# Keeping part of the input in SBUF between two passes, with the rest streamed through small slots

## The chip, the cores and the metric

One core of a Trainium2 chip. The metric is the device time of one execution in microseconds.

## The reference

```python
# x: (1, 384, 384, 384) bf16, channels last; w1d: (1,) bf16
g = jnp.einsum("bhwc->bc", x) / (H * W)     # mean of each channel
s = sigmoid(g * w1d[0])                     # k = 1: one weight for all channels
return x * s[:, None, None, :]
```

Every output needs a sum over the whole of x, so x (113 MB) has to pass through the core before the first output can be made. The four buffers that the kernel has in SBUF hold 25.2 MB of it.

## The kernel before

The 147,456 rows of 384 channels are cut in 18 tiles of 128 partitions x 64 rows, 6.29 MB each (48 KiB per partition). Four buffers hold one tile each. In the first pass TensorE sums each tile into PSUM by 64 matmuls with a matrix of ones. In the second all 18 tiles are loaded again, multiplied in place on VectorE and stored. Cuts are marked `# ...`.

```python
T = 18; n = 64; nbufs = 4; NL = 2 * T
# SyncE: all loads of both passes, in one loop
for i in range(NL):
    t = i % T; b = i % nbufs; k = i // nbufs
    if k >= 1:
        # wait until PE (first pass) or the store (second pass) has freed bufs[b]
        # ...
    sp.dma_start(bufs[b][:, :], xt[t]).then_inc(sem_ld[b], 16)

# TensorE: for each tile, once loaded
for r in range(n):
    ins = pe.matmul(psum_sums, ones_mat, bufs[b][:, r*C:(r+1)*C], start=..., stop=...)
ins.then_inc(sem_pe, 1)

# ScalarE: after the last tile
act.activation(s_b, psum_sums, Sigmoid, scale=wb_sb).then_inc(sem_sb, 1)
for t in range(T):
    act.wait_ge(sem_mul, t + 1)
    act.dma_start(ot[t], bufs[b][:, :]).then_inc(sem_st[b], 16)

# VectorE
for t in range(T):
    dve.wait_ge(sem_ld[b], 16 * (k + 1))      # t == 0 also waits for sem_sb
    dve.tensor_tensor(buf3, buf3, s_bc, mult).then_inc(sem_mul, 1)   # 128 x 24576
```

## Time and profile before

| | before |
|---|---|
| time | 798.71 us, median of 4 runs (798.19 to 798.87) |
| span of the profiled run | 796.1 us |
| HBM read, written | 226.5 MB, 113.2 MB |
| DMA share in both passes | 1.00, at 431 GB/s |
| VectorE busy | 233.4 us (29%) |

The span is the time from the first to the last instruction in the profile; the measured time of that same run was 797.84, 1.7 us more. The DMA share is the mean busy share of the core's 16 DMA engines. The prediction below shows the lines themselves.

### The profile page before, as it was taken

The page shows a single profiled execution, that of the slowest core. Times are in us where ns is not written, and L with a number is a line of the kernel's source. Part 1 is how long each engine was busy: PE and PEld are TensorE (multiplying, and loading weights), DVE is VectorE, ACT ScalarE, POOL GpSimd, SP SyncE. Part 2 cuts the span into 40 slices and gives each one's busy share as a digit, 9 for nine tenths or more (in the row PEclk, how much of TensorE's full clock was granted, in tenths as well). Part 3 has the DMA queues.
Part 4 walks back from the last instruction along what each step waited for, and adds up shares of the span by engine and source line. Part 5 has one row for each costly group of instructions (what it writes and reads, how often), then busy time and mean ns, then how long its engine had stood idle before and what let it go on. Part 6 is the DMA issues. An engine that isn't in the chain of part 4 may idle for free.

```text
span 796.1 us, 2417 instructions
## 1 busy us (share of the span) xinstructions
PE 209.6 (26%) x1153; PEld 117.8 (15%) x1153; DVE 233.4 (29%) x19; ACT 2.1 (0%) x3; POOL 0.5 (0%) x6
## 2 busy tenths in 40 slices
PE   0977887877878800000000000000000000000000
PEld 0534544544534400000000000000000000000000
DVE  0000000000000066624624623633632641651560
ACT  0000000000000000000000000000000000000000
POOL 0000000000000000000000000000000000000000
PEclk9989989989989965555555555555555555555555
DMA  9999999999999999999999999999999999999997
GB/s 385 436 435 431 433 435 428 428 432 433 428 430 433 428 432 435 435 435 435 427 425 435 430 435 432 427 435 427 435 425 430 427 435 435 435 432 435 432 395 326
DMA packets 7787, 339.89 MB, mean 427 GB/s; under 512 B 866, under 2 KB 866, under 8 KB 866
## 3 DMA queue, kind: packets, MB, share of 16 engines
q1 hardware_dynamic: 5186, 226.49, 66.3%
q10 hardware_dynamic: 2592, 113.25, 32.9%
q8 instruction: 9, 0.15, 0.1%
HBM read 226.49 MB, written 113.25 MB: 427 GB/s over the span
## 4 chain that ended last, share of the span: by engine, by line
another core or an unknown queue 33%; DMA 30%; DVE 28%; PE 7%; SPq 0%; issue 0%
DMA buf<-in_x_dram 30%; DVE buf L129 28%; PE psum_sums L101 7%; SPq L82 0%; SPq L70 0%
## 5 line engine op out<-in xcount | busy, mean ns | idle before, releaser
L129 DVE TENSOR_TENSOR buf<-buf,s_b 128x24576 bf16<-128x24576 bf16 x18 | 233.2, 12958 | 540.9 <-DMA buf<-in_x_dram 540.9
L101 PE MATMUL psum_sums<-buf,ones_mat 128*128 128x384 bf16 x1152 | 209.4, 347 | 66.5 <-DMA buf<-in_x_dram 66.5
L101 PEld LDWEIGHTS psum_sums<-buf,ones_mat 128*128 128x128 bf16 x1152 | 117.7, 103 | 157.9 <-DMA buf<-in_x_dram 73.1
L142 ACT ACTIVATE s_b<-psum_sums,wb_sb 128x384 bf16<-128x384 f32 x1 | 0.6, 580 | 275.5 <-PE psum_sums L101 275.5
L136 ACT ACT_TABLE_LOAD x1 | 1.3, 1283 | 0.7 <-PEq L169 0.7
L113 DVE TENSOR_SCALAR wb_sb<-psum_w 128x1 f32<-128x1 f32 x1 | 0.2, 159 | 2.2 <-PE psum_w L88 2.2
L88 PE MATMUL psum_w<-w_sb,ones_row 1*128 1x1 bf16 x1 | 0.2, 182 | 2.0 <-DMA w_sb<-in_w1d_dram 2.0
L88 PEld LDWEIGHTS psum_w<-w_sb,ones_row 1*128 1x128 bf16 x1 | 0.1, 100 | 2.0 <-DMA w_sb<-in_w1d_dram 2.0
L65 POOL MEMSET ones_mat<- 128x128 bf16 x1 | 0.2, 204 | 0.3 <-POOLq L169 0.3
L136 ACT ACTIVATE junk<-wb_sb 1x1 f32<-1x1 f32 x1 | 0.2, 202 | 0.4 <-DVE wb_sb L113 0.4
L66 POOL MEMSET ones_row<- 1x128 bf16 x1 | 0.2, 194 | 0.0
L169 POOL MEMSET const-bfloat16-1.0<- 128x1 bf16 x1 | 0.1, 106 | 0.0
L169 POOL MEMSET const-float32-0.0<- 128x1 f32 x1 | 0.1, 103 | 0.2 <-issue 0.2
L169 POOL MEMSET const-float32-1.0<- 128x1 f32 x1 | 0.1, 103 | 0.0
L169 POOL MEMSET const-uint8-127<- 128x1 uint8 x1 | 0.1, 103 | 0.0
## 6 DMA issues: line engine op xcount, KB each, us to landing
buf<-in_x_dram SPq DMA_DIRECT2D x36, 6144.0 KB, 49.0
out_dram<-buf ACTq DMA_DIRECT2D x18, 6144.0 KB, 50.6
w_sb<-in_w1d_dram SPq DMA_DIRECT2D x1, 0.0 KB
```

Source lines behind the costliest of these rows:

```text
L65: pool.memset(ones_mat[:, :], 1.0)
L66: pool.memset(ones_row[:, :], 1.0).then_inc(sem_ones, 1)
L88: pe.matmul(psum_w[:, 0:1], ones_row[0:1, :], w_sb[0:1, 0:1], start=True, stop=True,).then_inc(sem_wmm, 1)
L101: ins = pe.matmul(psum_sums[:, :], ones_mat[:, :], bufs[b][:, r * C:(r + 1) * C], start=(t == 0 and r == 0), stop=(t == T - 1 and r == n - 1),
L113: dve.tensor_scalar(wb_sb[:, 0:1], psum_w[:, 0:1], 1.0 / float(HW), None, mybir.AluOpType.mult,).then_inc(sem_wb, 1)
L129: dve.tensor_tensor(buf3, buf3, s_bc, mybir.AluOpType.mult).then_inc(sem_mul, 1)
L136: act.activation(junk[0:1, 0:1], wb_sb[0:1, 0:1], mybir.ActivationFunctionType.Sigmoid,)
L142: act.activation(s_b[:, :], psum_sums[:, :], mybir.ActivationFunctionType.Sigmoid, scale=wb_sb[:, 0:1],).then_inc(sem_sb, 1)
L169: nc = _bacc.Bacc("TRN2", target_bir_lowering=False, num_devices=1)
```

## The change

The first pass ends with tiles 14 to 17 in the four buffers. The change keeps them there instead of reading them again. The remainder of x must still be streamed through something, so an extra buffer of 16 rows and the first 48 rows of tile 14's buffer become four slots of 16 rows. All second-pass work is done in pieces of 16 rows (1.57 MB): first 13 resident pieces, which are only multiplied and stored, then 59 streamed ones. The last tile of the first pass is loaded in four quarters, so that TensorE need not wait for the whole of it. The diff, cut to its core:

```diff
-_NBUFS = 4
+_H = 16
+_N_STREAM = 4
+extra = es.enter_context(nc.sbuf_tensor("extra", [P, piece * C], bf16))
+slots = [extra[:, i * h * C:(i + 1) * h * C] for i in range(piece // h)]
+while len(slots) < _N_STREAM:
+    slots.append(pbuf[:, cut * C:(cut + h) * C]); cut += h
 # SyncE
-for i in range(NL): ...                       # 36 loads of a tile
+for t in range(T):                            # 18 tiles, the last in quarters
+    if t >= nb: sp.wait_ge(sem_pe, t - nb + 1)
+    # ...
+for u, (src, _d) in enumerate(stream):        # 59 pieces
+    s = u % ns
+    if u == n_extra: sp.wait_ge(sem_pe, part + 1)   # tile 14 has been summed
+    if u >= ns: sp.wait_ge(sem_st[s], 16 * (u // ns))
+    sp.dma_start(slots[s], src).then_inc(sem_sl[s], 16)
 # TensorE
+if t == T - 1 and r % piece == 0:
+    pe.wait_ge(sem_last[r // piece], 16)
 # VectorE: 13 resident pieces, then 59 streamed ones, 128 x 6144 each
-dve.tensor_tensor(buf3, buf3, s_bc, mult)
+for buf, r, k, _d in res:            dve.tensor_tensor(v, v, sbc(k), mult)
+for u in range(len(stream)): # ...   dve.tensor_tensor(v, v, sbc(h), mult)
 # ScalarE: stores of the same pieces in the same order
```

More of the change, by code (lines that the diff above doesn't have):

```diff
@@ L20, in bass_standalone__channel_attn_eca__vision_kernel @@
     n = _N_ROWS
-    nbufs = _NBUFS
+    h = _H
+    piece = 16
+    nb = 4
     assert S % (P * n) == 0
@@ L24, in bass_standalone__channel_attn_eca__vision_kernel @@
     HW = H * W
-    xt = x.rearrange("b h w c -> (b h w) c").rearrange(
-        "(t p k) c -> t p (k c)", p=P, k=n
-    )
-    ot = out.rearrange("b h w c -> (b h w) c").rearrange(
-        "(t p k) c -> t p (k c)", p=P, k=n
-    )
+    xr = x.rearrange("b h w c -> (b h w) c")
+    orr = out.rearrange("b h w c -> (b h w) c")
+    xt = xr.rearrange("(t p k) c -> t p (k c)", p=P, k=n)
+    ot = orr.rearrange("(t p k) c -> t p (k c)", p=P, k=n)
+    xs = xr.rearrange("(t p k) c -> t p (k c)", p=P, k=h)
+    os_ = orr.rearrange("(t p k) c -> t p (k c)", p=P, k=h)
     w2 = w1d.rearrange("(a b) -> a b", a=1)
-    NL = 2 * T
     with ExitStack() as es:
@@ L44, in bass_standalone__channel_attn_eca__vision_kernel @@
         psum_w = es.enter_context(nc.psum_tensor("psum_w", [P, 1], mybir.dt.float32))
-        sem_ld = [es.enter_context(nc.semaphore(f"sem_ld{i}")) for i in range(nbufs)]
-        sem_st = [es.enter_context(nc.semaphore(f"sem_st{i}")) for i in range(nbufs)]
+        bufs = [
+            es.enter_context(nc.sbuf_tensor(f"buf{i}", [P, n * C], mybir.dt.bfloat16))
+            for i in range(nb)
+        ]
+        extra = es.enter_context(nc.sbuf_tensor("extra", [P, piece * C], mybir.dt.bfloat16))
+        part = T - nb
+        pbuf = bufs[part % nb]
+        slots = [extra[:, i * h * C:(i + 1) * h * C] for i in range(piece // h)]
+        cut = 0
+        while len(slots) < _N_STREAM:
+            slots.append(pbuf[:, cut * C:(cut + h) * C])
+            cut += h
+        ns = len(slots)
+        n_extra = piece // h
+        stream = [(xs[u], os_[u]) for u in range(part * n // h)]
+        for r in range(0, cut, h):
+            stream.append((xt[part][:, r * C:(r + h) * C], ot[part][:, r * C:(r + h) * C]))
+        res = []
+        for t in range(part, T):
+            r = cut if t == part else 0
+            while r < n:
+                k = min(piece, n - r)
+                res.append((bufs[t % nb], r, k, ot[t][:, r * C:(r + k) * C]))
+                r += k
+        sem_ld = [es.enter_context(nc.semaphore(f"sem_ld{i}")) for i in range(nb)]
+        n_last = n // piece
+        sem_last = [es.enter_context(nc.semaphore(f"sem_la{i}")) for i in range(n_last)]
+        sem_sl = [es.enter_context(nc.semaphore(f"sem_sl{i}")) for i in range(ns)]
+        sem_st = [es.enter_context(nc.semaphore(f"sem_st{i}")) for i in range(ns)]
+        sem_rst = es.enter_context(nc.semaphore("sem_rst"))
         sem_wdma = es.enter_context(nc.semaphore("sem_wdma"))
@@ L53, in bass_standalone__channel_attn_eca__vision_kernel, with sbc @@
         sem_mul = es.enter_context(nc.semaphore("sem_mul"))
-        bufs = [
-            es.enter_context(nc.sbuf_tensor(f"buf{ib}", [P, n * C], mybir.dt.bfloat16))
-            for ib in range(nbufs)
-        ]
-        n_st_slot = [sum(1 for i in range(T, NL) if i % nbufs == b) for b in range(nbufs)]
+        def sbc(k):
+            return s_b[:, None, :].broadcast_to([P, k, C])
         with nc.Block() as block:
@@ L70, in _ @@
                 sp.dma_start(w_sb[:, :], w2[0:1, 0:1]).then_inc(sem_wdma, 16)
-                for i in range(NL):
-                    t = i % T
-                    b = i % nbufs
-                    k = i // nbufs
-                    if k >= 1:
-                        prev = i - nbufs
-                        if prev < T:
-                            sp.wait_ge(sem_pe, prev + 1)
-                        else:
-                            j = sum(1 for ii in range(T, prev + 1) if ii % nbufs == b)
-                            sp.wait_ge(sem_st[b], 16 * j)
-                    sp.dma_start(bufs[b][:, :], xt[t]).then_inc(sem_ld[b], 16)
+                for t in range(T):
+                    b = t % nb
+                    if t >= nb:
+                        sp.wait_ge(sem_pe, t - nb + 1)
+                    if t < T - 1:
+                        sp.dma_start(bufs[b][:, :], xt[t]).then_inc(sem_ld[b], 16)
+                    else:
+                        for q in range(n_last):
+                            lo, hi = q * piece * C, (q + 1) * piece * C
+                            sp.dma_start(
+                                bufs[b][:, lo:hi], xt[t][:, lo:hi]
+                            ).then_inc(sem_last[q], 16)
+                for u, (src, _d) in enumerate(stream):
+                    s = u % ns
+                    if u == n_extra:
+                        sp.wait_ge(sem_pe, part + 1)
+                    if u >= ns:
+                        sp.wait_ge(sem_st[s], 16 * (u // ns))
+                    sp.dma_start(slots[s], src).then_inc(sem_sl[s], 16)
             @block.tensor
@@ L95, in _ @@
                 for t in range(T):
-                    b = t % nbufs
-                    k = t // nbufs
-                    pe.wait_ge(sem_ld[b], 16 * (k + 1))
+                    b = t % nb
+                    if t < T - 1:
+                        pe.wait_ge(sem_ld[b], 16 * (t // nb + 1))
                     ins = None
                     for r in range(n):
+                        if t == T - 1 and r % piece == 0:
+                            pe.wait_ge(sem_last[r // piece], 16)
                         ins = pe.matmul(
@@ L119, in _ @@
                 ).then_inc(sem_wb, 1)
-                s_bc = s_b[:, None, :].broadcast_to([P, n, C])
-                for t in range(T):
-                    i = T + t
-                    b = i % nbufs
-                    k = i // nbufs
-                    dve.wait_ge(sem_ld[b], 16 * (k + 1))
-                    if t == 0:
-                        dve.wait_ge(sem_sb, 1)
-                    buf3 = bufs[b][:, :].rearrange("p (k c) -> p k c", k=n)
-                    dve.tensor_tensor(
-                        buf3, buf3, s_bc, mybir.AluOpType.mult
+                dve.wait_ge(sem_sb, 1)
+                for t in range(part, T - 1):
+                    dve.wait_ge(sem_ld[t % nb], 16 * (t // nb + 1))
+                for q in range(n_last):
+                    dve.wait_ge(sem_last[q], 16)
+                for buf, r, k, _d in res:
+                    v = buf[:, r * C:(r + k) * C].rearrange("p (k c) -> p k c", k=k)
+                    dve.tensor_tensor(
+                        v, v, sbc(k), mybir.AluOpType.mult
+                    ).then_inc(sem_mul, 1)
+                for u in range(len(stream)):
+                    s = u % ns
+                    dve.wait_ge(sem_sl[s], 16 * (u // ns + 1))
+                    v = slots[s].rearrange("p (k c) -> p k c", k=h)
+                    dve.tensor_tensor(
+                        v, v, sbc(h), mybir.AluOpType.mult
                     ).then_inc(sem_mul, 1)
@@ L147, in _ @@
                 ).then_inc(sem_sb, 1)
-                for t in range(T):
-                    i = T + t
-                    b = i % nbufs
-                    act.wait_ge(sem_mul, t + 1)
-                    act.dma_start(ot[t], bufs[b][:, :]).then_inc(sem_st[b], 16)
-                for b in range(nbufs):
-                    if n_st_slot[b] > 0:
-                        act.wait_ge(sem_st[b], 16 * n_st_slot[b])
+                j = 0
+                for buf, r, k, dst in res:
+                    j += 1
+                    act.wait_ge(sem_mul, j)
+                    act.dma_start(dst, buf[:, r * C:(r + k) * C]).then_inc(sem_rst, 16)
+                for u, (_s, dst) in enumerate(stream):
+                    s = u % ns
+                    j += 1
+                    act.wait_ge(sem_mul, j)
+                    act.dma_start(dst, slots[s]).then_inc(sem_st[s], 16)
+                act.wait_ge(sem_rst, 16 * len(res))
+                for s in range(ns):
+                    act.wait_ge(sem_st[s], 16 * len(range(s, len(stream), ns)))
 _INS = ['x', 'w1d']
```

## The prediction

> **What bounds the kernel now.** I began with the page's slices and its DMA lines, since a kernel that reads x twice and writes it once has only a multiplication per element to do.
>
> ```profile
> PE 209.6 (26%) x1153; PEld 117.8 (15%) x1153; DVE 233.4 (29%) x19; ACT 2.1 (0%) x3; POOL 0.5 (0%) x6
> ...
> DMA  9999999999999999999999999999999999999997
> GB/s 385 436 435 431 433 435 428 428 432 433 428 430 433 428 432 435 435 435 435 427 425 435 430 435 432 427 435 427 435 425 430 427 435 435 435 432 435 432 395 326
> DMA packets 7787, 339.89 MB, mean 427 GB/s; under 512 B 866, under 2 KB 866, under 8 KB 866
> ...
> HBM read 226.49 MB, written 113.25 MB: 427 GB/s over the span
> ```
>
> No engine is busy for a third of the span, while the DMA row is full from the first slice to the last but one, at the same rate in both passes. 427 GB/s over 796.1 us is all 339.9 MB: x read twice (2 x 113.25), the result written once. Next I read the chain in order of time, to get the period of the second pass:
>
> ```profile
> 705.49 0.02 issue
> 705.51 12.96 DVE buf L129
> 718.47 16.01 another core or an unknown queue
> 734.48 0.02 issue
> 734.50 12.96 DVE buf L129
> 747.46 16.02 another core or an unknown queue
> 763.48 0.02 issue
> 763.50 12.96 DVE buf L129
> ```
>
> A multiplication starts every 29.0 us and takes 12.96, so VectorE rests 16 us of each period. One period loads 6.29 MB and stores 6.29 MB: 12.58 MB / 29.0 us = 434 GB/s. The chain gives VectorE 28% of the span, but only because its line stands between one transfer and the next; with both queues kept full, a faster VectorE would gain nothing. Last, the windows over the first pass, the second, and the two parts of the end (columns: the window, its length, busy us of PE, PEld, DVE, ACT, POOL, clock, DMA share, GB/s):
>
> ```profile
> 2.00:264.00 262.00, 197.98 (x1084) 111.15 (x1085) 0.16 (x1) 0.22 (x2) 0.00 (x0) 0.92 1.00 431
> 310.00:764.00 454.00, 0.00 (x0) 0.00 (x0) 195.81 (x17) 0.00 (x0) 0.00 (x0) 0.50 1.00 431
> 764.00:777.00 13.00, 0.00 (x0) 0.00 (x0) 12.46 (x1) 0.00 (x0) 0.00 (x0) 0.50 0.80 348
> 777.00:797.00 20.00, 0.00 (x0) 0.00 (x0) 0.00 (x0) 0.00 (x0) 0.00 (x0) 0.50 0.75 324
> ```
>
> DMA share is 1.00 in both passes. Only at the end, from the last load's landing at 763.5, are the engines partly idle: 0.20 x 13 + 0.25 x 20 = 7.6 us. So the time is bytes over about 434 GB/s, plus a small head and tail.
>
> [...] The new pieces are 1.57 MB[...]. The trace has no transfer of that size, but it shows that a completion costs nothing while others are queued: 6.29 MB transfers end every 14.5 us in the first pass, with no idle share between. [...] the change needs 4 x 48 + 12 = 204 KiB plus about 1.5 for the small tensors[...].
>
> **The change part by part.** Call 16 rows per partition a piece: 128 x 12288 B = 1.573 MB, a quarter of a tile. x has 18 x 4 = 72 pieces.
>
> Removed: the last four tiles stay in their buffers after the first pass, except the first 48 rows of tile 14, whose place serves with the extra buffer as four streaming slots. Resident are 16 - 3 = 13 pieces; 14 x 4 + 3 = 59 are read again. Saved: 13 x 1.573 = 20.4 MB of 339.7, or 6.0%. At 434 GB/s that is 47.1 us of DMA time, all of it on the bounding resource.
>
> Added: smaller packets. The packet records of the trace have one packet per partition: 49152 B in 1815 ns (median), and the 4-byte semaphore write at the end of each transfer in 9 ns. Eight packets per DMA engine and one semaphore write make 8 x 1815 + 9 = 14.53 us per tile, which is the 14.5 us at which tiles land. My estimate for a 12288 B packet takes 9 ns as fixed and the rest as bytes: 1806/4 + 9 = 460 ns; a piece takes 8 x 460 + 9 = 3.69 us, against 3.63 for a quarter tile: 1.7% more.
>
> The sum of DMA time: 17 whole tiles x 14.53 = 247.0 us. Pieces: 4 (the last tile comes in four) + 59 loads + 72 stores = 135 x 3.69 = 498.2. Together 745.2; with 2.0 us before the first data, 747.2. The same sum for the kernel before is 54 x 14.53 + 2.0 = 786.6 against a span of 796.1, so 9.5 us lie beside it: 7.6 in the tail and some 2 in slow packets.
>
> Moved: the seam between the passes. The last load lands near 265 us, PE then needs one piece (16 matmuls at 10.57/64 = 0.165 us = 2.6 us) and not a whole tile, the sigmoid 0.6, [...] the issue about 1: the first store begins some 8 us after the last load. Meanwhile the four streaming loads stand in the queue (the extra buffer is free from the start, the three others once PE has done tile 14), 4 x 3.69 = 14.8 us of work. No bubble. Then 13 resident pieces: VectorE makes one per 3.36 + 0.05, DMA stores one per 3.69, so the store queue never empties, though by only 8%.
>
> Streaming: a slot's round is load 3.69, [...] multiplication 3.36, issue about 1, store 3.69, [...]: some 16 us unloaded [...]. DMA needs 2 x 3.69 = 7.4 us per piece, four slots 29.5. 29.5 against 16: almost twice what it takes to keep DMA busy. About three transfers should stand in the queues at any time.
>
> The tail: after the last load one multiplication of 3.4 us instead of 13, with earlier stores still running beside it, so the 2.6 us of idle DMA there shrink to 1 or less; the last transfer's stragglers and receipt remain, 3 us. Slow packets: 2 us before, [...] I take 4 in all. Span: 747.2 + 4 + 4 = 755. The measured time is 798.71 - 796.1 = 2.6 above the span: 758.
>
> **The rivals.** (1) Turnover of slots becomes the bound[...] I give it 4% in full and expect at most a trace of it. (2) Engines drift apart. In the landing records of the second pass, the 16 engines' parts of one load come up to 10 us apart, which buffers of 6.29 MB absorb; four slots hold about 11 us of work per engine, so a straggler may hold up a slot and leave others dry. A loss of 3% in the 400 us of streaming would be 12 us: 770. (3) VectorE bounds the resident stretch: if a piece took 4 us instead of 3.4, 13 x 0.3 = 4 us more: 762. The trace's fixed durations (all 18 at 12.96) speak against it. (4) Smaller packets cost nothing: 135 x 0.06 = 9 us less: 749. (5) The saved reads were hidden anyway: then 797; a DMA share of 1.00 in the very stretch where they fell excludes it.
>
> **Range and chances.** Rivals 2 and 3 push up, 4 down; so 748 to 774 about 758. Within 2% of 798.7 (above 783) it comes only if streaming loses over 25 us, rival 2 doubled or rival 1 in part: 6%. Slower by 2% needs rival 1 in full: 2%.
>
> **What would show it.** HBM read should be 206.1 MB, written 113.25. The DMA row should be full from end to end, the rate 425 to 430 in the second pass; 12288 B packets near 460 ns. VectorE: 72 multiplications of 3.36 us. The first resident store soon after 275 us, streaming loads landed near 281, resident stores done near 326, then 7.4 us per piece. I am wrong if the DMA row shows 7s and 8s in the streaming stretch with VectorE and both queues waiting by turns (rival 1 or 2), or if the rate falls at a full share (a packet cost mis-sized).

The trace of the kernel before has no multiplication of 16 rows and does not show a slot's round of 16 us. r_after has 3358 ns for the first (59 streamed pieces, mean), the 3.36 of the text. The 16 was the author's estimate; the steps that the text names with their times add up to 11.7 us. In the kernel before, the last load lands at 763.48, 0.06 us after its last packet, and the multiplication starts at 763.50; the last store lands 0.33 us after its last packet. Below, e3 gives the steps of a whole round.

## The result, and the profile after

Ratios are the mean time of one kernel's fast runs over that of the other's of the same rounds, so not quite the ratio of the medians that are quoted.

| | before | changed |
|---|---|---|
| median | 798.42 us (15 runs) | 751.59 us (10 runs, 8 fast) |
| fast runs | 796.09 to 800.29 | 750.15 to 754.56 |
| ratio of fast runs | 1 | 0.9413, 95% interval 0.9401 to 0.9426 |

The change is 5.9% faster, within the range. Executions over 1.5% slower than the fastest of the same kernel are left out of the means. Two of the ten runs were slow: 778.1 us at a mean granted clock of 0.571, which is the run that was profiled, and one of 1204.0 us at a clock of 1.0. The second was not profiled and never came again; nothing here explains it. So the same kernel was profiled again (the run r_after), and that profile is read here.

Its page, in the rows that answer to those shown for before:

```profile
PE 209.7 (28%) x1153; PEld 118.0 (16%) x1153; DVE 240.5 (32%) x73; ACT 2.1 (0%) x3; POOL 0.5 (0%) x6
...
DMA  9999999999999999999999999999999999999998
GB/s 377 435 438 423 440 433 423 440 438 420 435 438 423 413 404 426 423 428 400 429 430 430 430 430 430 431 430 430 431 430 430 430 430 430 431 430 430 429 430 373
DMA packets 21902, 319.47 MB, mean 426 GB/s; under 512 B 2434, under 2 KB 2434, under 8 KB 2434
...
HBM read 206.05 MB, written 113.25 MB: 425 GB/s over the span
```

The DMA row is as full as before, the mean rate is the same (426 against 427 GB/s), and 20.4 MB less were read. 20.4 of 339.9 MB is 6.0%; the span went from 796.1 to 750.5, 5.7%. The change left the kernel's bound where it was and gave it less to do.

The streaming stretch, from the timeline (start, length, what, and in brackets the idle time of the engine before it and what ended it):

```profile
609.04 3.36 DVE L175 TENSOR_TENSOR extra<-extra,s_b 128x6144 bf16<-128x6144 bf16 x1 [3.96 <-DMA extra<-in_x_dram]
...
616.37 3.36 DVE L175 TENSOR_TENSOR buf<-buf,s_b 128x6144 bf16<-128x6144 bf16 x1 [3.98 <-DMA buf<-in_x_dram]
...
631.02 3.36 DVE L175 TENSOR_TENSOR buf<-buf,s_b 128x6144 bf16<-128x6144 bf16 x1 [3.97 <-DMA buf<-in_x_dram]
...
638.34 3.36 DVE L175 TENSOR_TENSOR extra<-extra,s_b 128x6144 bf16<-128x6144 bf16 x1 [3.97 <-DMA extra<-in_x_dram]
```

The extra buffer comes round every 29.30 us, four pieces: 7.32 us per load and store of 1.573 MB each, 430 GB/s. The waits of VectorE, all of 3.96 to 3.98 us, are worth noting: the four slots are evenly spread. This will be different with fewer slots.

The same kernel by windows: first pass, seam, resident pieces, streaming, end (columns as in the prediction).

```profile
2.00:264.00 262.00, 197.12 (x1078) 110.60 (x1079) 0.16 (x1) 0.23 (x2) 0.00 (x0) 0.92 1.00 430
264.00:284.00 20.00, 12.48 (x77) 7.31 (x75) 6.87 (x3) 0.58 (x1) 0.00 (x0) 0.87 0.96 404
284.00:330.00 46.00, 0.00 (x0) 0.00 (x0) 46.00 (x15) 0.00 (x0) 0.00 (x0) 0.50 1.01 424
330.00:735.00 405.00, 0.00 (x0) 0.00 (x0) 181.66 (x55) 0.00 (x0) 0.00 (x0) 0.50 1.01 429
735.00:751.00 16.00, 0.00 (x0) 0.00 (x0) 5.85 (x2) 0.00 (x0) 0.00 (x0) 0.50 0.82 349
```

In the resident stretch VectorE is busy for all 46 us, yet DMA stays full. The idle part of DMA is small: about 0.04 x 20 at the seam and 0.18 x 16 = 2.9 us at the end, where the kernel before had 7.6. The prediction added up packet times, so the queue lines matter too (queue, packets, MB, time of the packets as a share of 16 engines' span), of the kernel before, then of r_after:

```profile
q1 hardware_dynamic: 5186, 226.49, 66.3%
q10 hardware_dynamic: 2592, 113.25, 32.9%
```

```profile
q1 hardware_dynamic: 11522, 206.05, 64.2%
q10 hardware_dynamic: 10368, 113.25, 35.6%
```

In sum 99.2% of 796.1 us, 789.7, and 99.8% of 750.5 us, 749.0.

### The profile page after: what moved, and what is told of

Its sections match the earlier page's. It is cut to its first block, busy times and chain, and to the rows that moved or that the text cites.

```text
span 776.3 us, 2572 instructions
## 1 busy us (share of the span) xinstructions
PE 283.2 (36%) x1153; PEld 139.2 (18%) x1153; DVE 240.5 (31%) x73; ACT 2.1 (0%) x3; POOL 0.5 (0%) x6
## 3 DMA queue, kind: packets, MB, share of 16 engines
q1 hardware_dynamic: 11522, 206.05, 62.1%
HBM read 206.05 MB, written 113.25 MB: 411 GB/s over the span
## 4 chain that ended last, share of the span: by engine, by line
DMA 50%; PE 36%; DVE 13%; issue 0%; ACT 0%; SPq 0%
PE psum_sums L142 36%; DMA buf<-in_x_dram 26%; DMA out_dram<-buf 24%; DVE buf L175 7%; DVE buf L168 5%; DVE extra L175 0%; ACT s_b L188 0%; SPq L102 0%
## 5 line engine op out<-in xcount | busy, mean ns | idle before, releaser
L142 PE MATMUL psum_sums<-buf,ones_mat 128*128 128x384 bf16 x1152 | 283.1, 432 | 16.6 <-DMA buf<-in_x_dram 16.6
L175 DVE TENSOR_TENSOR buf<-buf,s_b 128x6144 bf16<-128x6144 bf16 x44 | 147.6, 3358 | 162.7 <-DMA buf<-in_x_dram 162.7
L142 PEld LDWEIGHTS psum_sums<-buf,ones_mat 128*128 128x128 bf16 x1152 | 139.1, 121 | 160.1 <-DMA buf<-in_x_dram 16.7
L168 DVE TENSOR_TENSOR buf<-buf,s_b 128x6144 bf16<-128x6144 bf16 x13 | 42.6, 3354 | 300.1 <-ACT s_b L188 300.1
L175 DVE TENSOR_TENSOR extra<-extra,s_b 128x6144 bf16<-128x6144 bf16 x15 | 50.4, 3358 | 65.1 <-DMA extra<-in_x_dram 65.1
```

The costliest lines, as they stand in the source:

```text
L142: ins = pe.matmul(psum_sums[:, :], ones_mat[:, :], bufs[b][:, r * C:(r + 1) * C], start=(t == 0 and r == 0), stop=(t == T - 1 and r == n - 1),
L168: dve.tensor_tensor(v, v, sbc(k), mybir.AluOpType.mult).then_inc(sem_mul, 1)
L175: dve.tensor_tensor(v, v, sbc(h), mybir.AluOpType.mult).then_inc(sem_mul, 1)
```

## The experiments

The theory: the gain is the 20.4 MB not read again, at the rate of the DMA engines, and nothing else in the change matters much. The rival: finer pieces, with their shorter seam and end, make part of it. Behind that stood three terms of the prediction that could be tested alone: that four slots are ample, that small packets cost 1.7%, and that the seam is closed by the quartered last tile.

**Repeats (r_after, r_after2, r_after3).** The unaltered kernel: r_after beside e1, e2 and e3, r_after2 beside e5, e6 and e7, r_after3 beside e9. e8 and e4 ran on another chip without a repeat of their own.

> The changed kernel once more, unaltered, for a profile in the fast state (the first one fell in the slow state). Both theories: 751 to 753 us, ratio to before 0.941. If bytes over rate explain it (theory A), the fast profile shows a DMA share of 1.00 from the seam to the last load, 12288 B packets at 460 ns, and a period of 7.4 us per piece in the streaming stretch; PE done with the last tile about 3 us after its last quarter lands and no dip of the DMA row at the seam. If finer pieces themselves give part of the gain (theory B: a shorter tail and seam), the part of the saving that the bytes do not explain shows at the end and at the seam.

> The changed kernel once more as the base of the next three on the same chip: 751 to 752 us in its fast runs.

> The changed kernel as the base of the next run on the same chip: 751 to 752 us.

Measured: 751.82, 751.93 and 751.46 us, ratios 0.9408, 0.9409 and 0.9410. The packet records give 460 ns for a 12288 B packet (median), as predicted. The "no dip at the seam" part of the first expectation failed in r_after, and only there; see below.

**e1: the same pieces, nothing kept.**

```diff
-stream = [(xs[u], os_[u]) for u in range(part * n // h)]
+stream = [(xs[u], os_[u]) for u in range(T * n // h)]
-for t in range(part, T):          # resident pieces
+for t in range(0):                # none; the 48 extra rows of tile 14 dropped too
```

> The changed kernel with nothing kept: all 72 pieces are read again through the same four slots of 16 rows, so pieces, slots and packets stay and only the 13 saved loads come back. Theory A (bytes): 13 x 3.69 = 48 us more than the changed kernel, 800 us, as slow as the kernel before or 1 to 2 us slower. Theory B (the finer pieces and shorter seam give a good part of it): clearly under 798, 785 or less.

Measured: 798.17 us (798.05 to 798.75), ratio to before 0.9991, interval 0.9970 to 1.0012. This undoes only the saved reads and keeps slots, pieces, packets and quarters. The whole gain went, so the rival falls: finer pieces by themselves are worth nothing here, on balance (what they cost in packets and what they gain at the end cancel; e6 takes the packets alone). From 751.82 it is 46.4 us for 13 loads, 3.57 us each; I had said 48.

**e6: the packet cost by itself**, on the kernel before: each tile's transfer issued as four, waits per tile kept (counts of 64 for 16).

```diff
-sp.dma_start(bufs[b][:, :], xt[t]).then_inc(sem_ld[b], 16)
+for q in range(4):                # stores likewise
+    lo, hi = q * n * C // 4, (q + 1) * n * C // 4
+    sp.dma_start(bufs[b][:, lo:hi], xt[t][:, lo:hi]).then_inc(sem_ld[b], 16)
```

> The kernel before with each tile's load and store issued as four transfers of 16 rows (12288 B packets), buffers, multiplications and waits per tile as they were: the packet cost by itself. With 9 ns per packet as predicted: 216 x 3.69 - 54 x 14.53 = 12 us more, 811. With the 7.32 us per pair that the streaming stretch of the changed kernel shows (3.66): 6 us more, 805. If smaller packets cost nothing: 799.

Measured: 802.24 us, ratio to before 1.0041 (1.0025 to 1.0057). The net cost is 3.7 us and not 12. Its windows, over the first and the second pass of before:

```profile
2.00:264.00 262.00, 191.96 (x1057) 107.72 (x1058) 0.16 (x1) 0.22 (x2) 0.00 (x0) 0.93 1.01 423
310.00:764.00 454.00, 0.00 (x0) 0.00 (x0) 199.68 (x16) 0.00 (x0) 0.00 (x0) 0.50 1.01 430
```

423 against 431 GB/s in the first pass, 430 against 431 in the second, where the loss nearly vanishes. The packets did get longer as forecast: the queue lines of this run's page add up to 67.0 + 33.2 = 100.2% of its 800.2 us, 801.8 us, against 789.7 before, 12.1 us more. But a share above 1 says that packets overlap, so that their durations may not simply be added. Counted in the packet records, the packets under way beyond 16 at once (the core has 16 DMA engines) add up to 6.9 us per engine here and 1.6 in the kernel before, which takes back 5.3 us. Some 3 us more come back; the engines stand idle less at the end, 0.15 x 24 = 3.6 us from 777 on (share 0.85) where the kernel before has 7.6, another thing that this edit changes.

**e7, e2, e3: five, three and two slots.** One constant, `_N_STREAM`, is 5, 3 or 2. Each slot less keeps one more piece resident.

> Five streaming slots, 12 pieces resident. If four slots already keep DMA full: one load more, 3.66 us longer, 755 us. If four slots lose something to turnover: under 754, perhaps under the changed kernel.

> Three streaming slots of 16 rows in place of four; one more piece stays resident. Theory A: a slot's round of about 16 us unloaded is under 3 x 7.38 = 22.1 us, so DMA stays full and the time falls by one load, 3.7 us, to 748. Rival (slots are already short; a transfer takes about 13 us from issue to landing): streaming slows, 760 us or more.

> Two streaming slots; two more pieces resident, 57 read again. Theory A with my round of 16 us: 2 x 7.38 = 14.8 is under 16, so turnover binds, at least 8.0 us per piece: 55 x 0.6 = 33 more less 7.4 for the saved loads, 777 us or more, up to 830 when the two slots wait for each other, with a DMA share of 0.8 to 0.92 in the streaming stretch. [...]

| slots | resident pieces | time, us | note |
|---|---|---|---|
| 5 | 12 | 754.09 (753.83 to 755.09) | |
| 4 | 13 | 751.93 (750.63 to 752.51) | r_after2 |
| 3 | 14 | 783.78 (767.75 to 792.99) | three of four count as slow, see text |
| 2 | 15 | 816.30 (815.32 to 817.46) | ratio to before 1.0217 |

Three slots miss my expectation of 748 badly. Three of its four runs count as slow; their clocks (0.650 to 0.655) are those of the undisturbed kernel before (0.649 to 0.654), so I take the spread as the kernel's own; the profiled one, 785.1 us, is among them, and its first pass has a clock of 0.92, as r_after has. The one run that counts as fast, 767.75, is still 16 us above four slots. The two-slot runs, all fast, show the mechanism without this doubt. Two slots and three slots (340 to 500 us, then 500 to 760), by windows, one fence for each kernel:

```profile
400.00:700.00 300.00, 0.00 (x0) 0.00 (x0) 120.73 (x36) 0.00 (x0) 0.00 (x0) 0.50 0.93 371
```

```profile
340.00:500.00 160.00, 0.00 (x0) 0.00 (x0) 70.52 (x21) 0.00 (x0) 0.00 (x0) 0.50 1.01 424
500.00:760.00 260.00, 0.00 (x0) 0.00 (x0) 107.91 (x33) 0.00 (x0) 0.00 (x0) 0.50 0.98 384
```

Two slots run at 371 GB/s with the engines idle for 7% of the time. Three hold 424 GB/s for a while and then fall to 384 at a share of 0.98. The timelines show how the slots stand to each other. Two slots, then three:

```profile
620.03 3.36 DVE L175 TENSOR_TENSOR extra<-extra,s_b 128x6144 bf16<-128x6144 bf16 x1 [9.85 <-DMA extra<-in_x_dram]
...
623.71 3.36 DVE L175 TENSOR_TENSOR buf<-buf,s_b 128x6144 bf16<-128x6144 bf16 x1 [0.33 <-DMA buf<-in_x_dram]
...
636.94 3.36 DVE L175 TENSOR_TENSOR extra<-extra,s_b 128x6144 bf16<-128x6144 bf16 x1 [9.87 <-DMA extra<-in_x_dram]
```

```profile
626.88 3.36 DVE L175 TENSOR_TENSOR extra<-extra,s_b 128x6144 bf16<-128x6144 bf16 x1 [10.73 <-DMA extra<-in_x_dram]
...
631.00 3.36 DVE L175 TENSOR_TENSOR buf<-buf,s_b 128x6144 bf16<-128x6144 bf16 x1 [0.77 <-DMA buf<-in_x_dram]
...
637.98 3.36 DVE L175 TENSOR_TENSOR buf<-buf,s_b 128x6144 bf16<-128x6144 bf16 x1 [3.62 <-DMA buf<-in_x_dram]
```

VectorE's waits are no longer even: about 10 us, then almost none. The slots have closed up into a convoy: they load one after the other, then store one after the other. With two slots the packet records show the engines all on loads, then a gap of about a microsecond (from the last load until the first store's data), then all on stores. A load issued at 611.64 has no packet before 615, when the other slot's store is done. The round of 16.9 us is two loads (7.9 us of packets), the gap, and two stores (8.6) one after the other. That it lies near the 16 that I had reckoned for one unloaded slot is chance, and the expectation of 777 to 830 came out by its second half, the two slots waiting for each other, not by the turnover. The same trace has the steps of one slot: a store that nothing stands before moves its first data 0.84 us after its issue and has landed after 5.1, 308 GB/s for its 1.573 MB, and a load lands some 0.4 us after its last packet. An estimate from these, with 0.96 us from the kernel's first load issue to its data, is 5.1 + 3.4 + 5.1 = 13.6 us for an unloaded round of 16 rows. So my 16 was too high, and three slots, 22 us of work, had even more margin on paper.

In the three-slot run's bad stretch the idle share is only 2%, so most of the loss is not idleness: the mean load packet takes 538 ns there (460 median; 13% are over 690), where the same kernel before 500 us had 467. With two slots it is the store packets that stretch, to 513. The kernels with four slots or more of 16 rows show none of this: by the stores' queue lines r_after and five slots have some 463 and 461 ns a store packet on the mean, and in the first profile of the changed kernel (slow), from 500 to 760 us, load and store packets both take 460. In the same stretch of the three-slot run the 16 parts of one transfer land up to 5.1 us apart, before 500 us at most 1.7: engines drift apart there. Why packets stretch when the slots run in convoy, and whether the drift is cause or effect, is not settled.

Five slots, 754.09, cost 2.2 us more than four, where one load more should cost 3.66; as an expectation this decides nothing, since 754 lies on the border. The windows over the seam of that run:

```profile
264.00:284.00 20.00, 9.95 (x62) 5.76 (x59) 9.40 (x3) 0.58 (x1) 0.00 (x0) 0.81 1.01 424
284.00:330.00 46.00, 0.00 (x0) 0.00 (x0) 46.00 (x15) 0.00 (x0) 0.00 (x0) 0.50 1.01 430
```

r_after has 404 and 424 GB/s in these windows, so one might think that a fifth hidden load fills the seam. But r_after2, the four-slot run of the same batch, has 426 and 429, and no hole to fill. The missing 1.5 us are not explained; the runs of four slots alone spread over 1.9 us. In streaming (400 to 700 us) both run at 430 GB/s, and that shows that four slots were enough.

**e8 and e4: slots of 8 rows**, `_H = 8`, with six slots (the same 48 rows as three of 16) and with four.

> Six streaming slots of 8 rows: the same 48 rows of slots and the same 14 resident pieces as the three slots of 16 rows, which came out at 768 to 793 us and lost DMA share after some 200 us of streaming. If the loss comes from the few, long transfers (all slots bunch at one stage, and one multiplication of 3.36 us and two landings are a large part of a round), six short ones keep the DMA share at 1.00: one load of 16 rows less than the changed kernel, 3.7 us, and 6144 B packets, by (1806/8 + 5) ns about 0.03 us more per 8 rows, 116 x 2 x 0.03 = 6 us: 750 to 755. If it comes from the bytes that the slots hold, the same loss: 765 or more.

> Four streaming slots of 8 rows, 15 pieces resident. Two loads of 16 rows less than the changed kernel (7.3 us), packets 6 us more: 750 if DMA stays full. [...] the same proportion as three slots of 16 rows (16 against 22), which failed; so I expect a loss as there, 765 to 800 us.

Measured: six slots 754.80 us (754.23 to 756.76, ratio 0.9450); four slots 787.18 us over all four runs, its fast ones 783.71 to 789.07, ratio 0.9835. Six and four, by windows; the profiled run of the latter was its longest, 813.2 us, and counts as slow (clock 0.646; 0.92 in the first pass, as elsewhere), so its 365 GB/s overstates the loss. Its fast runs, at 784 to 789 where a full DMA row would give 750, show that there is one:

```profile
400.00:700.00 300.00, 0.00 (x0) 0.00 (x0) 141.58 (x82) 0.00 (x0) 0.00 (x0) 0.50 1.02 425
```

```profile
400.00:700.00 300.00, 0.00 (x0) 0.00 (x0) 122.13 (x70) 0.00 (x0) 0.00 (x0) 0.50 0.99 365
```

So it is not the bytes that the slots hold: 48 rows in six slots keep DMA full, 48 rows in three do not. Nor is it their number: four of 16 rows do, four of 8 do not. What sorts all of them is the DMA work of one round of all slots against one slot's unloaded round. That round is an estimate from the measured steps above: 13.6 us with 16 rows; with 8, 2 x (1.4 + 1.85) + 1.76 = 8.3, from the 1.4 us that the lone store took beyond its 3.7 of packets, half of those packets, and the 1.76 us of a multiplication in e8.

| slots | work of a round over one slot's round | DMA |
|---|---|---|
| 2 x 16 | 14.6 / 13.6 = 1.1 | 371 GB/s |
| 3 x 16 | 22 / 13.6 = 1.6 | 424, later 384 (run counts as slow) |
| 4 x 8 | 15 / 8.3 = 1.8 | 365 (run counts as slow) |
| 4 x 16 | 29.3 / 13.6 = 2.2 | 430 |
| 6 x 8 | 22 / 8.3 = 2.7 | 425 |

The last four rows are the point: 1.6 and 1.8, which should suffice on paper, do not, and 2.2 does. Where between them the border lies is not shown, and five kernels do not make it a rule.

**e5 and e9: the seam.** e5 loads the last tile whole; e9 loads the last two in quarters.

```diff
-if t < T - 1:        # e5: "t < T", and no waits on sem_last
+if t < T - 2:        # e9: sem_last has 8 entries, used by tiles 16 and 17
```

> The last tile loaded whole and not in four quarters. My prediction has PE done one quarter (2.6 us) after the last load; the fast profile of the changed kernel shows PE running without a break through tiles 16 and 17 and ending at 276.5, some 10 us after the last load, with a dip of the DMA row of about 1.3 us at 279 to 282. If PE's backlog from the whole tile 16 sets the end (my theory now), the quarters buy almost nothing: the sigmoid starts within 2 us of 276.5 and the time is 0 to 2 us longer. If the prediction's step holds (quarters save 8 us of PE), the seam opens by about 8 us: 757 us or more.

> The last two tiles in quarters and not the last alone. If PE ends late in the changed kernel because tile 16 landed whole and PE still had all of it to do, PE now starts tile 16 with its first quarter and ends about 3 to 5 us after the last load, the sigmoid starts near 270 in place of 276.5, the dip of the DMA row at 279 to 282 goes, and the time falls by the dip, 1 to 2 us, to 750. If PE ends late for another reason, nothing moves.

Measured: e5 755.15 us (753.29 to 756.10), ratio 0.9449 (0.9431 to 0.9468), 3.2 us longer than r_after2. e9 750.51 us against 751.46 for r_after3; ratios 0.9398 (0.9385 to 0.9411) and 0.9410 (0.9398 to 0.9423), a difference of 0.9 us that the intervals do not resolve. The timelines of r_after, e5 and e9, in TensorE's last work and the sigmoid:

```profile
252.95 23.54 PE L142 MATMUL psum_sums<-buf,ones_mat 128*128 128x384 bf16 x128 [3.98 <-DMA buf<-in_x_dram]
276.52 0.58 ACT L188 ACTIVATE s_b<-psum_sums,wb_sb 128x384 bf16<-128x384 f32 x1 [273.96 <-PE psum_sums L142]
```

```profile
267.70 12.99 PE L140 MATMUL psum_sums<-buf,ones_mat 128*128 128x384 bf16 x64 [3.98 <-DMA buf<-in_x_dram]
280.73 0.58 ACT L184 ACTIVATE s_b<-psum_sums,wb_sb 128x384 bf16<-128x384 f32 x1 [278.15 <-PE psum_sums L140]
```

```profile
239.79 32.50 PE L142 MATMUL psum_sums<-buf,ones_mat 128*128 128x384 bf16 x187
272.32 0.58 ACT L188 ACTIVATE s_b<-psum_sums,wb_sb 128x384 bf16<-128x384 f32 x1 [269.74 <-PE psum_sums L142]
```

In r_after, TensorE starts tile 16 at 252.95, when the whole of it has landed, and runs through 128 matmuls without a break: it is not waiting for the quarters of tile 17 but is behind them. By the landing records the last quarter is there at 267.7, and TensorE ends 8.8 us later. With the last tile whole, the sigmoid comes 4.2 us later still and the DMA row opens at the seam (the windows give a share of 0.16 from 280 to 284, where r_after has 0.84). With two tiles quartered, TensorE starts tile 16 earlier but then has three tiles in a row to do (the window cuts off the first few matmuls; 187 take 32.5 us), and still ends near 272. So my guess that quarters buy "0 to 2 us" was low (3.2), the prediction's 8 us much too high, and the most to be had at this seam is about 1 us.

The dip itself was no fixed feature. In r_after the granted clock was 0.50 for the first 5 us of tile 16, and the 128 matmuls took 23.54 us; in r_after2 and r_after3 it was 1.00 and they took 20.97, the sigmoid started at 273.95 and 273.64, and there was no dip. (In e5 the half clock fell on the last tile, 0.50 from 268 to 272, 12.99 us in place of 10.57, so 2.4 us of its late sigmoid are the clock's.) So e9, whose base is r_after3, had no dip to remove.

No version beats the changed kernel by a resolved amount; e9, at 750.5, is the lowest.

## Why the prediction was right, and where it was not

**Bound and bytes: right.** HBM read 206.05 MB (206.1 predicted), a full DMA row, and e1 shows that the reads alone make the gain. Rivals 1 (turnover) and 5 (hidden reads) did not happen; rival 3 (VectorE bounding the resident stretch) neither, with 13 multiplications of 3.35 us in that stretch and DMA full (share 1.01 from 284 to 330 in r_after). Rival 4, small packets for nothing, came nearest: 751.6 lies closer to its 749 than to 758 (135 x 0.06 is 8 and not 9, so it should have said 750).

**758 against 751.6.** The packet times were right: 745.2 us, with 4 for slow packets 749.2, and the queue lines of r_after give 749.0. What was wrong was to add them up as if each engine had one packet at a time: "a piece takes 8 x 460 + 9 = 3.69 us". Packets overlap, by the count used for e6 for 4.7 us of r_after (1.6 in the kernel before), and a streaming pair takes 7.32 us and not 7.38. That is most of the 6.4 us, and e6 shows the same fault: 12.1 us more packet time, 5.3 more overlap. Two small things make up the rest: I set one run's span against other runs' median, 2.6 us, where within one run it is 1.8; and r_after is 0.7 us slower than the median. 4.7 + 0.8 + 0.7 = 6.2. The end, taken at 4 us, shows 2.9, and the seam of r_after, taken as closed, lost about 1; these cancel. "I take 4 in all" for slow packets was luck: by the packet records the time above the median is 4.1 us in r_after, but 4.5 in the kernel before, not 2, so the shallower queues did not raise it.

**"PE then needs one piece (2.6 us)": wrong in mechanism, harmless in time.** TensorE was still at work on the backlog from tile 16, and the first store was issued at 280.5 us, not "soon after 275". The four hidden loads, 14.8 us of DMA work, covered most of it in r_after and all of it in r_after2 and r_after3.

**"Almost twice what it takes": wrong.** The ratio 29.5 against 16 was right as arithmetic, the reading that everything above 1 is margin was not. With three slots, 22 us of work against 13.6 by the measured steps (1.6), they close up into a convoy, and 31 us or more are lost in the median, 16 in the one run that counts as fast. The 16 was too high besides: the measured steps give 13.6, and the two-slot trace has 1.4 for all that a lone store takes beyond its packets (5.1 - 3.7). Rival 2, engines drifting apart, was the nearest thought but did not occur in the changed kernel: with four slots the landings of one transfer lie about 1 us apart, not 10. With three they lie up to 5.1 apart. The change sits one slot above a cliff, which the prediction did not see.

## What to carry to other kernels

When DMA is full from end to end, count the bytes: data that happens to lie in SBUF when a pass ends is worth its reload time, at the measured rate, to within a microsecond or two. But the slots that feed the rest should not be taken down to the number that a sum of latencies allows; here rings whose work was 1.6 and 1.8 times one slot's round, estimated from the measured steps, lost 2% at the least (three slots, its one fast run) and 4.5% (four short slots, fast runs) against the changed kernel, while 2.2 times ran at 430 GB/s, as fast as five slots. And a tile cut finer to shorten a wait helps only if the engine that waits is not still busy with the tile before it.
